# Two layers of linear attention and a Mish MLP: load order and turns at the start, one block's statistics, and the order of the last products

## The chip, the cores and the metric

The kernel runs on one core of a Trainium2 chip. A core has TensorE (PE in the profile, with its weight loads as PEld), VectorE (DVE), ScalarE (ACT), GpSimd (POOL), SyncE (SP, which here issues the DMAs) and 16 DMA engines. SBUF is the working memory of 128 partitions; PE writes its results to PSUM, eight banks of 512 fp32 columns. The metric is the device time of one execution in microseconds; less is better.

## The reference

Input `x` has 2048 rows of 640. Two layers run one after the other with the same weights. Each is an attention part and a dense part with a layer norm ahead and a residual addition behind:

```python
for layer in range(2):
    x = x + attention(layernorm(x))
    x = x + mlp(layernorm(x))

# attention, 32 heads of 20
q, k, v = split_heads(x @ wqkv)
pq, pk = q @ w_phi, k @ w_phi                       # per head, 20 x 20
phi = concat(softmax(p), softmax(-p))               # 40 features, for q and for k
kv, z = phi_k^T @ v, sum(phi_k)                     # over all 2048 rows
o = (phi_q @ kv) / (phi_q . z + 1e-6)
return o @ wo

# mlp
h = x @ w1 + b1                                     # 1536 wide
return (h * tanh(softplus(h))) @ w2
```

All is fp32.

## The kernel before

Rows are taken in `NB` = 8 blocks of 256, each as two row tiles of 128 (`t` = 0, 1). Every large product is made of three: an operand is split into a high part (`ACT` copies it rounded) and a low part (DVE or POOL subtracts), and high by high, high by low and low by high are added up in PSUM. A row of 640 results lies in two halves of 320 columns, `c` = 0, 1, a PSUM bank each. PSUM is given out as two double tiles `mm` (`mm_tile`, two banks each) and four single ones (`one_tile`).

A layer has three stages. `attend_first` runs over the blocks and makes keys, values and queries, and their features; `attend_second` runs over them again for the attention's output; `dense` runs over (block, `pr`) steps, 12 per block. In step `pr`, `hidden` makes two of the twelve times 128 hidden columns, `mish` brings them through the activation on ACT, DVE and POOL to `ah` and `al` (high and low parts), and two steps later `contract` multiplies them by `w2`. `end` adds the row block `xt` and stores it.

The first layer's start is written out by hand, on all engines. PE first makes `TURNS` transposes of the identity matrix (L543), whose result nobody reads. SP issues the loads: the first row tile (L549), the first part of the feature map `w_phi` as block diagonals (`load_phi`, L256), the raw transposed query weights in six tiles (`load_raw`, L247), and the rest of the map (three loads, L258 and L260). `differences` (DVE, L266) turns the map into differences to each head's first feature. `fold` (PE, L273) multiplies raw weights and map to folded weights, five products per raw tile, one per 128 rows of the weights; `fold_parts` splits them into high (ACT, L282) and low (DVE, L284). Tile 0 of the raw weights is folded for all five, then tile 1 for two of them, then PE turns the first normalised rows (L355), and then come the rest of tile 1 and tile 2. The values' weights `wv` (L138) and the keys' raw weights are loaded behind.

Further on in the same stretch `fold_keys` folds the keys' weights; their low parts are written `parts[2]` and `parts[3]` in an order of their own. Then come the values of the first block, whose PSUM tiles are those that `parts[3]` held. `norm_stats` (L290, L292) and `norm_scale` (POOL L300 and L301, DVE L305) make mean and scale of a block.

Behind this, from the second block on, only PE's and SP's order is written for a while, or nobody's: a planner that simulates the time puts the instructions in order. `tc.issue_after(ins)` tells it that what is made inside stands behind `ins` on the engine of `ins`. So stand the third block's statistics: `fetch_normed(b + 1)` at `b == 1` stands behind `ready`, which is DVE's last shift of the second block's `norm_scale`:

```python
with tc.issue_after(ready):
    xt = fetch_normed(b + 1)
```

At the end of the last layer, the last `contract` takes its 24 products with the two hidden columns outermost (`j`, then `t`, `c` and the three parts), and the planner may still move them. `end` adds the four results of 128 x 320 one by one on DVE (L994) and stores row tile 0 whole (L998) and row tile 1 in halves (L996).

Of the kernel before, what the change touches and what calls it, by code (L numbers as in the profile page):

```python
# [8 lines left out]
F32 = mybir.dt.float32  # L9
F32R = mybir.dt.float32r  # L10
AF = mybir.ActivationFunctionType
ALU = mybir.AluOpType
# [4 lines left out]
P = 128  # L17
# [6 lines left out]
KF = F // P  # L24
BT = 2
BLK = BT * P
NB = S // BLK
NT = S // P
G = 11
HC = D // 2  # L30
# [7 lines left out]
SKEW = 2  # L38
V_ORDER = (0, 1, 4, 2, 3)
FOLD = (6, 6, 6, 6, 4, 4)  # L40
TURNS = 20
LAYERS = 2
LN_EPS = 1e-5
DEN_EPS = 1e-6
# [7 lines left out]
def kernel(  # L52
# [13 lines left out]
    nc = tc.nc  # L66
# [8 lines left out]
    def mm_tile():  # L75
        return psum.tile([P, 2, 512], F32, tag="mm", name="mm", bufs=2)

    def one_tile():
        return psum.tile([P, 512], F32, tag="one", name="one", bufs=4)
# [4 lines left out]
    def x_tile():  # L84
        return work.tile([P, BT, D], F32, tag="x", name="xt", bufs=2)
# [19 lines left out]
    stats = const.tile([P, NB, 2, BT], F32, name="stats")  # L105
# [10 lines left out]

    last_act = [None]
    written = [False]
    last_scale = [None]
    last_recip = [None]  # L120

    def act(*args, **kw):
# [51 lines left out]
    def r2_wide(j, dtype=F32R):  # L174
        return wts.tile([P, 2, D], dtype, tag=f"r2{j}", name=f"r2{j}")
# [60 lines left out]
    def load_raw(which, ts=range(6)):  # L236

        raw = []
        for t in ts:
            r0 = which * D + DH * sum(FOLD[:t])  # L240
            if t < 5:
                r = wts.tile([P, D], F32, tag=f"r2{'hl'[which]}{5 + t}", name=f"raw{which}{t}")
            else:
                r = row_tile() if which else r2_wide(10, F32)[:, 0]

            n = P if t < 5 else DH * FOLD[t]
            nc.sync.dma_start(r[:n], wqk_t[r0:r0 + n, :])  # L247
            raw.append(r)
        return raw

    def load_phi(bd, late):

        flat = bd.rearrange("p t c -> p (t c)")
        src = phi_bd.rearrange("p t c -> p (t c)")
        if not late:
            nc.sync.dma_start(flat[:, :360], src[:, :360])  # L256
            return
        nc.sync.dma_start(flat[:, 360:600], src[:, 360:600])  # L258
        for n, rows in enumerate((slice(80, 120), slice(0, 40))):
            nc.sync.dma_start(flat[40 * n:40 * n + 40, 600:680], src[rows, 560:640])  # L260
# [17 lines left out]
    def fold_parts(ws, ps, k, c, which=(0, 1)):  # L278
        n0, n1 = (0, 18 * DF) if c == 0 else (18 * DF, FW)
        hi, lo = ws[k][0][:, n0:n1], ws[k][1][:, n0:n1]  # L280
        if 0 in which:
            nc.scalar.activation(hi, ps[:, :n1 - n0], AF.Copy)  # L282
        if 1 in which:
            nc.vector.tensor_tensor(lo, ps[:, :n1 - n0], hi.bitcast(F32), op=ALU.subtract)  # L284

    def norm_stats(t, xt):

# [7 lines left out]
    def norm_scale(b, mvs, t0=0, later=False):  # L295

        n = len(mvs)
        ve = work.tile([P, BT], F32, tag="ve", name="ve", bufs=2)
        for t in range(n):
            nc.gpsimd.tensor_scalar(ve[:, t:t + 1], mvs[t][:, 1:2], LN_EPS, 1.0, op0=ALU.add, op1=ALU.mult)  # L300
        nc.gpsimd.tensor_tensor(stats[:, b, 0, t0:t0 + n], ve[:, :n], neg_half[:, :n], op=ALU.pow)  # L301

        def shifts():
            for t in range(n):
                last_scale[0] = nc.vector.tensor_scalar(stats[:, b, 1, t0 + t:t0 + t + 1], mvs[t][:, 0:1],  # L305
                                                        stats[:, b, 0, t0 + t:t0 + t + 1], -1.0,
                                                        op0=ALU.mult, op1=ALU.mult).ins
        if later:
            return shifts
        shifts()  # L310
# [56 lines left out]
    def row_tile():  # L367
        return work.tile([P, D], F32, tag="xn", name="xn", bufs=4)

    def normed_rows(b, xt):  # L370

        xn = [row_tile() for _ in range(BT)]
        normalize(b, xn, [xt[:, t, :] for t in range(BT)])
        return xn
# [4 lines left out]
    def normalize(b, dst, src):  # L379
        for t in range(BT):  # L380
            act(dst[t], src[t], AF.Identity, bias=stats[:, b, 1, t:t + 1], scale=stats[:, b, 0, t:t + 1])
# [87 lines left out]
    def fetch(x_src, b, xt=None):  # L469
        xt = x_tile() if xt is None else xt  # L470
        nc.sync.dma_start(xt, row_block(x_src, b))
        return xt

    def attend_first(layer, x_src, first):
# [62 lines left out]
        if first is None:  # L537
            E = mybir.EngineType
            with tc.manual_schedule(engines={E.PE, E.SP, E.Activation, E.DVE, E.Pool}):
                written[0] = True  # L540
                ps = one_tile()
                for _ in range(TURNS):
                    nc.tensor.transpose(ps[:, :P], ident, ident)  # L543
                xt = x_tile()
# [3 lines left out]
                def fetch_first(t):  # L548
                    nc.sync.dma_start(xt[:, t], row_block(x_src, 0)[:, t])  # L549
# [8 lines left out]
                def query_parts(banks, c, ks):  # L558
                    for n in range(2):
                        for k in ks:  # L560
# [1 line left out]

                fetch_first(0)
                load_phi(bd, False)
                raw = load_raw(0, range(3))
                load_phi(bd, True)
                raw += load_raw(0, range(3, 6))
                fetch_first(1)
                q_ws = [r2_pair(k) for k in range(KD)]
                kv_ws = [r1_pair(k) for k in range(KD)]  # L570
# [2 lines left out]
                mvs = [norm_stats(0, xt)]  # L573
# [4 lines left out]
                                        op0=ALU.mult, op1=ALU.add)  # L578
# [17 lines left out]
                turned, last = one_tile(), one_tile()  # L596
# [9 lines left out]
                mvs = [norm_stats(1, xt)]  # L606
# [25 lines left out]
                raw = raw_k  # L632
# [15 lines left out]
                xt = fetch(x_src, 1)  # L648
                mvs = [norm_stats(t, xt) for t in range(BT)]
# [1 line left out]
                    for n in range(2):  # L651
                        parts[k](n)
                norm_scale(1, mvs)
                ready = last_scale[0]
                next(g1)
                parts[2](0)
                parts[3](0)
                parts[2](1)
                parts[3](1)
                nxt_rows = normed_rows(1, xt)  # L660
                next(g1)
                next(g0)
# [28 lines left out]
        for b in range(0 if layer else 1, NB):  # L691
            xts = nxt
            order = ("k0", "k1", "v0", "v1", "q0", "q1")
            if b == 0:
                order = ("v0", "k0", "k1", "v1", "q0", "q1")
            elif b == 1 and layer == 0:
                order = ("k0", "q0", "k1", "v0", "q1", "v1")
            elif b == NB - 1:
                order = ("k0", "k1", "v0", "v1", "q0")
            vs = [v_tile() for _ in range(BT)]  # L700
            for n, (kind, t) in enumerate(order):
                t = int(t)
# [6 lines left out]
                if b + 1 < NB:  # L709
                    if n == 0 and b == 1 and layer == 0:  # L710
                        with tc.issue_after(ready):
                            xt = fetch_normed(b + 1)
                    elif n == 0:
                        xt = fetch_normed(b + 1)
# [213 lines left out]
    def dense(x_src, x_dst, w1s, w2s, first, last):  # L928
        blocks = {0: first}
# [38 lines left out]
            nc.gpsimd.tensor_tensor(al[:, js], n, ah[:, js].bitcast(F32), op=ALU.subtract)  # L968

        def contract(b, pr, ah, al):  # L970
            if pr == 0:
                blocks[b][2] = [mm_tile() for _ in range(BT)]
            pys = blocks[b][2]
            order = [(t, j) for t in range(BT) for j in range(2)]
            if b == NB - 1 and pr == KF // 2 - 1:
                order = [(t, j) for j in range(2) for t in range(BT)]
            for t, j in order:
                sl = slice(t * P, (t + 1) * P)
                f = 2 * pr + j
                for c in range(2):  # L980
                    cs = slice(c * HC, (c + 1) * HC)
                    wh, wl = w2s[f][0][:, cs], w2s[f][1][:, cs]
                    for n, (l, r) in enumerate(((ah, wh), (ah, wl), (al, wh))):
                        nc.tensor.matmul(pys[t][:, c, :HC], l[:, j, sl], r,  # L984
                                         start=(f == 0 and n == 0), stop=(f == KF - 1 and n == 2))

        def end(b):
            xt, _, pys = blocks.pop(b)
            dst = row_block(x_dst, b)
            if last and b == NB - 1:  # L990
                for t in range(BT):
                    for c in range(2):
                        cs = slice(c * HC, (c + 1) * HC)
                        nc.vector.tensor_tensor(xt[:, t, cs], pys[t][:, c, :HC], xt[:, t, cs], op=ALU.add)  # L994
                        if t == BT - 1:
                            nc.sync.dma_start(dst[:, t, cs], xt[:, t, cs])  # L996
                    if t < BT - 1:
                        nc.sync.dma_start(dst[:, t], xt[:, t])  # L998
                return
            mvs = []  # L1000
            for t in range(BT):
                nc.vector.tensor_tensor(xt[:, t, :].rearrange("p (c d) -> p c d", c=2), pys[t][:, :, :HC],
                                        xt[:, t, :].rearrange("p (c d) -> p c d", c=2), op=ALU.add)
                if not last:
                    mvs.append(norm_stats(t, xt))
            if not last:
                norm_scale(b, mvs)
            nc.sync.dma_start(dst, xt)
            if not last:
                xn = [row_tile() for _ in range(BT)]  # L1010
                normalize(b, xn, [xt[:, t, :] for t in range(BT)])
                spill_turned(xn, n2_d[b])
# [13 lines left out]
        for i in range(len(steps) + SKEW):  # L1026
            if i < len(steps):
                b, pr = steps[i]
# [19 lines left out]
            if i <= KD:  # L1048
                with tc.issue_after(exps[0]):
                    w = next(last_w2)  # L1050
# [5 lines left out]
            if i >= SKEW:  # L1056
                b, pr = steps[i - SKEW]
# [5 lines left out]
    with tc.block(schedule_with_timeline_sim=True):  # L1063
        src, first = x, None
        for layer in range(LAYERS):
            last = layer == LAYERS - 1
# [5 lines left out]
            w2s = {}  # L1072
# [73 lines left out]
```

## Time and profile before

| | |
|---|---|
| median of 3 runs | 1357.73 us (1356.86 to 1359.12) |
| the profiled execution | 1358.86 us |
| its span | 1357.0 us |
| PE busy | 1349.5 us (99%) |
| DVE busy | 1069.5 us (79%) |
| ACT busy | 584.5 us (43%) |
| POOL busy | 469.3 us (35%) |
| bytes moved by DMA | 169.21 MB, mean 125 GB/s |

The span runs from the first to the last instruction of the program. A row of the timeline gives start and duration in us, engine, line of the kernel, operation, and tiles as out<-in, with the number of merged instructions; in brackets stands how long the engine was idle before, and what ended that. Products overlap in PE, so a row of several lasts longer than their number times their pace. `raw` are raw weights, `big` is here the feature map, `r1h`, `r1l`, `r2h` and `r2l` are weights in parts, `xth` and `xtl` turned rows in parts, `ol` the activated hidden columns.

### The profile page before, as it was taken

How to read it: one execution, taken by the hardware profiler on the slowest of the kernel's cores; microseconds unless marked ns; L12 is line 12 of the kernel's file. 1: busy time of each engine (PE TensorE's matmuls, PEld its weight loads, DVE VectorE, ACT ScalarE, POOL GpSimd, SP SyncE). 2: the span in 40 equal slices, each digit the busy share in tenths (PEclk: the TensorE clock that was granted, in tenths of full speed). 3: DMA queues.
4: the chain of work that ended last, by engine and by line, in shares of the span. 5: the costliest groups of instructions: out<-in, count | busy, mean ns of one | idle time of the engine just before them, and what ended most of it. 6: DMA issues, size and time to landing. Idle time of an engine off the chain costs nothing.

```text
span 1357.0 us, 30926 instructions
## 1 busy us (share of the span) xinstructions
PE 1349.5 (99%) x12886; PEld 1337.6 (99%) x12886; DVE 1069.5 (79%) x1810; ACT 584.5 (43%) x1039; POOL 469.3 (35%) x357
## 2 busy tenths in 40 slices
PE   9999999999999999999999999999999999999998
PEld 9999999999999999999999999999999999999998
DVE  6988788887787887778779888888768776676775
ACT  5443444222454545545444344332236444444443
POOL 3345644444222222222225556744441211111111
PEclk9999999999999999999999999999999999999999
DMA  9624335798614542334473534467964231233200
GB/s 337 183 41 78 81 60 124 186 287 285 192 36 94 117 117 73 60 102 109 133 238 72 115 72 76 82 159 233 301 238 117 79 87 26 85 98 98 73 26 20
DMA packets 350613, 169.21 MB, mean 125 GB/s; under 512 B 287225, under 2 KB 323817, under 8 KB 350473
## 3 DMA queue, kind: packets, MB, share of 16 engines
q1 hardware_dynamic: 350473, 167.23, 46.2%
q8 instruction: 101, 1.65, 0.5%
q14 instruction: 39, 0.32, 0.1%
HBM read 104.61 MB, written 62.59 MB: 123 GB/s over the span
## 4 chain that ended last, share of the span: by engine, by line
PE 98%; DVE 1%; DMA 0%; ACT 0%; issue 0%; SPq 0%; DVEq 0%; ACTq 0%
PE mm L417 28%; PE mm L984 25%; PE one L942 25%; PE one L417 13%; PE mm L802 3%; PE one L327 2%; PE one L502 2%; PE mm L273 0%; DMA raw<-in_wqk_t 0%; DVE r1l L284 0%; PE one L802 0%; DVE m L453 0%; DVE r L458 0%; DVE r L456 0%; PE one L273 0%
## 5 line engine op out<-in xcount | busy, mean ns | idle before, releaser
L984 PE MATMUL mm<-r2h,ol 128*128 128x320 f32 x1280 | 304.9, 309 | 0.0
L968 POOL TENSOR_TENSOR ol<-big,ol 128x512 fp32r<-128x512 f32 (+1 forms) x98 | 130.5, 1332 | 484.7 <-ACT ol L967 391.3
L942 PE MATMUL one<-xtl,r1h 128*128 128x256 f32 x960 | 268.6, 280 | 0.0
L942 PE MATMUL one<-xth,r1l 128*128 128x256 f32 x960 | 268.4, 280 | 0.0
L942 PE MATMUL one<-xth,r1h 128*128 128x256 f32 x960 | 266.3, 280 | 0.0
L984 PEld LDWEIGHTS mm<-r2h,ol 128*128 128x128 f32 x1280 | 219.4, 188 | 0.0
L984 PE MATMUL mm<-r2l,ol 128*128 128x320 f32 x640 | 197.6, 310 | 0.0
L417 PE MATMUL mm<-r1h,xth 128*128 128x304 f32 (+1 forms) x600 | 185.3, 309 | 0.0
L417 PE MATMUL mm<-r1h,xtl 128*128 128x304 f32 (+1 forms) x600 | 184.1, 307 | 0.0
L417 PE MATMUL mm<-r1l,xth 128*128 128x304 f32 (+1 forms) x600 | 183.9, 306 | 0.0
L942 PEld LDWEIGHTS one<-xtl,r1h 128*128 128x128 f32 x960 | 180.8, 188 | 0.0
L942 PEld LDWEIGHTS one<-xth,r1l 128*128 128x128 f32 x960 | 180.7, 188 | 0.0
L942 PEld LDWEIGHTS one<-xth,r1h 128*128 128x128 f32 x960 | 179.9, 188 | 0.0
L957 DVE TENSOR_SCALAR big<-big 128x512 f32<-128x512 f32 (+1 forms) x98 | 56.2, 573 | 112.1 <-ACT big L955 111.9
L466 POOL TENSOR_TENSOR big<-big,r 128x1280 f32<-128x1280 f32 x42 | 101.4, 2418 | 70.3 <-DVE r L465 46.1
L984 PEld LDWEIGHTS mm<-r2l,ol 128*128 128x128 f32 x640 | 120.4, 188 | 0.0
L955 ACT ACTIVATE big<-one,b1s 128x256 f32<-128x256 f32 x192 | 80.8, 467 | 91.7 <-PE one L942 90.8
L959 ACT ACTIVATE big<-big,two 128x512 f32<-128x512 f32 (+1 forms) x98 | 70.1, 716 | 115.2 <-DVE big L958 115.0
L967 ACT ACTIVATE ol<-big 128x512 fp32r<-128x512 f32 (+1 forms) x98 | 60.9, 621 | 133.4 <-DVE big L966 133.2
L417 PEld LDWEIGHTS mm<-r1h,xth 128*128 128x128 f32 x600 | 113.0, 188 | 0.6
L417 PEld LDWEIGHTS mm<-r1h,xtl 128*128 128x128 f32 x600 | 112.9, 188 | 0.4
L417 PEld LDWEIGHTS mm<-r1l,xth 128*128 128x128 f32 x600 | 113.0, 188 | 0.0
(171 smaller groups left out, 3121.1 us busy)
## 6 DMA issues: line engine op xcount, KB each, us to landing
big<-e_d SPq DMA_DIRECT2D x30, 640.0 KB, 6.4
x_d<-xt SPq DMA_DIRECT2D x23, 640.0 KB, 4.2
e_d<-r SPq DMA_DIRECT2D x88, 160.0 KB, 4.0
xt<-x_d SPq DMA_DIRECT2D x22, 640.0 KB, 5.9
n_d<-xn SPq DMA_DIRECT2D x176, 80.0 KB, 2.2
xt<-in_x SPq DMA_DIRECT2D x15, 640.0 KB, 4.4
xn<-x_d SPq DMA_DIRECT2D x28, 320.0 KB, 4.6
v<-n_d SPq DMA_DIRECT2D x30, 256.0 KB, 3.2
```

What stands on the lines that cost most here:

```text
L327: nc.tensor.transpose(ps[:, c, t * P:(t + 1) * P], self.rows[t][:, (c0 + c) * P:(c0 + c + 1) * P], ident)
L417: nc.tensor.matmul(ps[:, :w], a[:, sl], r, start=(k == 0 and n == 0), stop=(k == final and n == end))
L466: nc.gpsimd.tensor_tensor(eg, eg, r.unsqueeze(2).to_broadcast([P, 2 * H, DH]), op=ALU.mult)
L502: nc.tensor.matmul(kva[32 * q:32 * q + DH + 1, c:c + 2 * DH], v[:, (DH + 1) * h:(DH + 1) * (h + 1)], e[:, 2 * DH * h:2 * DH * (h + 1)], st ...
L802: nc.tensor.matmul(po[c][64 * q:64 * q + 64, GW * j:GW * j + w], phs[g][:n, s0:s0 + 64], kvb[:n, g, :w], start=True, stop=True)
L942: nc.tensor.matmul(ph[:, j, :], l, r, start=(n == 0), stop=(n == 3 * KD - 1))
L955: exps[0] = nc.scalar.activation(part(ta, 0)[:, j - js.start], ph[:, j, :], AF.Exp, bias=b1s[:, 2 * pr + j:2 * pr + j + 1]).ins
L957: nc.vector.tensor_scalar_min(e, e, E_CAP)
L959: nc.scalar.activation(r, n, AF.Ln, bias=two)
L967: nc.scalar.activation(ah[:, js], n, AF.Copy)
L968: nc.gpsimd.tensor_tensor(al[:, js], n, ah[:, js].bitcast(F32), op=ALU.subtract)
L984: nc.tensor.matmul(pys[t][:, c, :HC], l[:, j, sl], r, start=(f == 0 and n == 0), stop=(f == KF - 1 and n == 2))
```

## The change

Four edits. The number of turns at the start goes from 20 to 24. The three loads of the map's rest are issued behind the first raw tile instead of behind the third. `ready` becomes DVE's last low part of the keys' `parts[2]` and `parts[3]`, so that the third block's statistics stand behind it. In the last block of the last layer, row tile 1's second half gets a PSUM tile of its own (`one_tile`, held for the block's 12 steps), the last 24 products get a written order, row tile 0 first with the low parts of its second hidden column last, then the first half of row tile 1, then its second half, and `end` reads from the tile of its own.

```diff
-TURNS = 20
+TURNS = 24
...
-    last_scale = [None]
+    last_low = [None]
...
         if 1 in which:
-            nc.vector.tensor_tensor(lo, ps[:, :n1 - n0], hi.bitcast(F32), op=ALU.subtract)
+            last_low[0] = nc.vector.tensor_tensor(lo, ps[:, :n1 - n0], hi.bitcast(F32), op=ALU.subtract).ins
...
-                last_scale[0] = nc.vector.tensor_scalar(stats[:, b, 1, t0 + t:t0 + t + 1], mvs[t][:, 0:1],
-                                                        stats[:, b, 0, t0 + t:t0 + t + 1], -1.0,
-                                                        op0=ALU.mult, op1=ALU.mult).ins
+                nc.vector.tensor_scalar(stats[:, b, 1, t0 + t:t0 + t + 1], mvs[t][:, 0:1],
+                                        stats[:, b, 0, t0 + t:t0 + t + 1], -1.0, op0=ALU.mult, op1=ALU.mult)
...
-                raw = load_raw(0, range(3))
+                raw = load_raw(0, range(1))
                 load_phi(bd, True)
-                raw += load_raw(0, range(3, 6))
+                raw += load_raw(0, range(1, 6))
...
                 norm_scale(1, mvs)
-                ready = last_scale[0]
                 next(g1)
                 parts[2](0)
                 parts[3](0)
                 parts[2](1)
                 parts[3](1)
+                ready = last_low[0]
                 nxt_rows = normed_rows(1, xt)
...
         def contract(b, pr, ah, al):
+            final = last and b == NB - 1
             if pr == 0:
                 blocks[b][2] = [mm_tile() for _ in range(BT)]
+                if final:
+                    blocks[b].append(one_tile())
             pys = blocks[b][2]
-            order = [(t, j) for t in range(BT) for j in range(2)]
+
+            def product(t, j, c, n):
+                f = 2 * pr + j
+                l, w = ((ah, 0), (ah, 1), (al, 0))[n]
+                ps = blocks[b][3] if final and t == c == 1 else pys[t][:, c]
+                nc.tensor.matmul(ps[:, :HC], l[:, j, t * P:(t + 1) * P], w2s[f][w][:, c * HC:(c + 1) * HC],
+                                 start=(f == 0 and n == 0), stop=(f == KF - 1 and n == 2))
+
+            order = [(t, j, c, n) for t in range(BT) for j in range(2) for c in range(2) for n in range(3)]
             if b == NB - 1 and pr == KF // 2 - 1:
-                order = [(t, j) for j in range(2) for t in range(BT)]
...
+                order = [(t, j, c, n) for j in range(2) for t in range(BT) for c in range(2) for n in range(3)]
+                if final:
+                    order = ([(0, 0, c, n) for c in range(2) for n in range(3)] + [(1, 0, 0, n) for n in range(3)]
+                             + [(0, 1, c, n) for ns in ((0, 1), (2,)) for c in range(2) for n in ns]
+                             + [(1, 1, 0, n) for n in range(3)] + [(1, j, 1, n) for j in range(2) for n in range(3)])
+            with ExitStack() as written_order:
+                if final and pr == KF // 2 - 1:
+                    written_order.enter_context(tc.manual_schedule(engines={mybir.EngineType.PE}))
+                for o in order:
+                    product(*o)
...
-                        nc.vector.tensor_tensor(xt[:, t, cs], pys[t][:, c, :HC], xt[:, t, cs], op=ALU.add)
+                        ps = apart[0] if t == c == 1 else pys[t][:, c]
+                        nc.vector.tensor_tensor(xt[:, t, cs], ps[:, :HC], xt[:, t, cs], op=ALU.add)
```

More of the change, by code (lines that the diff above doesn't have):

```diff
@@ L970, in contract @@
         def contract(b, pr, ah, al):
+            final = last and b == NB - 1
             if pr == 0:
                 blocks[b][2] = [mm_tile() for _ in range(BT)]
+                if final:
+                    blocks[b].append(one_tile())
             pys = blocks[b][2]
-            order = [(t, j) for t in range(BT) for j in range(2)]
-            if b == NB - 1 and pr == KF // 2 - 1:
-                order = [(t, j) for j in range(2) for t in range(BT)]
[L977 to L985, printed above, removed]
+            def product(t, j, c, n):
[4 more added lines that the diff above has]
+                                 start=(f == 0 and n == 0), stop=(f == KF - 1 and n == 2))
@@ L987, in end @@
+            with ExitStack() as written_order:
[3 more added lines that the diff above has]
+                    product(*o)
         def end(b):
-            xt, _, pys = blocks.pop(b)
+            xt, _, pys, *apart = blocks.pop(b)
             dst = row_block(x_dst, b)
```

## The prediction

> **What bounds the kernel now.** I read the page first, then who waits for whom on PE, then the timeline of the three places that the diff touches. The page says that PE is busy nearly everywhere and that the chain that ended last is PE's own.
>
> ```profile
> PE 1349.5 (99%) x12886; PEld 1337.6 (99%) x12886; DVE 1069.5 (79%) x1810; ACT 584.5 (43%) x1039; POOL 469.3 (35%) x357
> ```
>
> ```profile
> PE 98%; DVE 1%; DMA 0%; ACT 0%; issue 0%; SPq 0%; DVEq 0%; ACTq 0%
> ```
>
> The waits of PE (engine, line, what it waited for, us in total, times, longest) show what little an edit could remove inside the span, beside PE's late start.
>
> ```profile
> PE one L273 <- DMA raw<-in_wqk_t: 0.6, 1, 0.6
> ...
> PE one L417 <- DVE r1l L284: 0.4, 1, 0.4
> ```
>
> In the steady stretch the chain (start, us, what) has a step of the dense layer as 30 hidden and 24 final products, 3.50 + 3.52 = 7.02 us, and a product of 320 columns at 3.52 / 24 = 0.147 us.
>
> ```profile
> 1331.47 3.50 PE one L942 x30
> 1334.97 3.52 PE mm L984 x24
> ```
>
> So no edit of this kind is worth tens of microseconds. What can be won is at the front, where PE waits and runs slowly, in one stall near 36 us, and behind the last product. The reader is to see in the next rows (start, duration, engine, line, tiles, count) that the same eight fold products take 1.92 us at 7.04 and 1.06 us at 11.32.
>
> ```profile
> 1.34 4.53 PE L543 MATMUL one<-ident 128*128 128x128 f32 x20 [1.34 <-POOL ident masks.py:199]
> 1.67 1.30 SPq L247 DMA_DIRECT2D raw<-in_wqk_t  x3
> 3.01 0.44 SPq L258 DMA_DIRECT2D big<-in_phi_bd  x1
> 3.49 0.71 SPq L260 DMA_DIRECT2D big<-in_phi_bd  x2
> ...
> 6.50 0.75 PE L273 MATMUL one<-big,raw 120*128 120x114 f32 x2 [0.63 <-DMA raw<-in_wqk_t]
> 7.04 1.92 PE L273 MATMUL mm<-big,raw 120*128 120x114 f32 x8
> ...
> 9.60 1.00 PE L355 MATMUL one<-ident,xn 128*128 128x128 f32 x5
> ...
> 11.32 1.06 PE L273 MATMUL mm<-big,raw 120*128 120x114 f32 x8
> ```
>
> The products' own durations (ns, minimum, median, most) are these.
>
> ```profile
> L273 PE MATMUL mm<-big,raw x70: 243/276/422, 7.0 to 31.3; 120*128 120x114 f32 x56, 80*128 80x76 f32 x14
> ```
>
> So one product follows the other after (1.92 - 0.42) / 7 = 0.214 us, and later after (1.06 - 0.28) / 7 = 0.112 us. The five turns of 9.60 would take 1.28 us at the slow pace and 0.72 at the fast one; with 1.00 the step lies among them, at about 10.2 us. PE ran at half pace for all of its first nine microseconds, the 20 turns included, although the page's clock row reads full speed.
>
> **Edits 1 and 2: 24 turns, late maps ahead of the second raw weights.** Four more turns cost 4 x 0.214 = 0.86 us of PE. The 20 end at 5.87, and as the next instruction can follow 0.21 before that, 24 let the first fold start at 5.87 - 0.21 + 0.86 = 6.52, where it starts at 6.50 today. They lie wholly in the wait for the first raw weights; if those land sooner, because only 138 KB of maps and no longer 640 KB of raw weights share the DMA engines with them, the turns cost what the landing gains. I count nothing for that.
>
> What the turns can bring is the pace. 4.3 us of unbroken turns (1.34 to 5.66) were not enough to raise it, and 3.7 us of work from 6.50 to 10.2 were. So the pace isn't counted from the first instruction. [...]
>
> [...]
>
> Then the ten products of the first raw tile: 1.8 slow ones to 6.9, 8.2 x 0.112 = 0.92 behind, done at 7.82. The second raw tile is wanted there; today it isn't wanted before 8.75. Its landing, with those of the third and the fourth, follows (KB, us from issue to landing; two issued with steps of 0.43 in the group of 1.67, at 2.1 and 2.5, the other behind the maps, at 4.2), and the DMA rate in the last column of the stretch.
>
> ```profile
> raw<-in_wqk_t SPq DMA_DIRECT2D x1, 320.0 KB, 5.4
> ```
>
> ```profile
> raw<-in_wqk_t SPq DMA_DIRECT2D x1, 320.0 KB, 5.8
> ```
>
> ```profile
> raw<-in_wqk_t SPq DMA_DIRECT2D x1, 320.0 KB, 6.0
> ```
>
> ```profile
> 7.50:8.50 1.00, 1.00 (x6) 1.00 (x6) 0.00 (x0) 0.00 (x0) 0.00 (x0) 1.00 1.05 391
> ```
>
> It lands at 7.5 today, the third at 8.3, the fourth at 10.2. On SP the three map loads now pass ahead of the second and third raw load, which are issued 0.44 + 0.71 = 1.15 us later; that alone doesn't move a landing that comes 5.4 us after the issue. 138 KB at 391 GB/s put it 0.35 us later. From above: between the landings of the third and the fourth lie 1.9 us for the maps and one raw tile that elsewhere takes 0.8 to 1.1 us, so the maps can cost 1.1 us. I take 0.45, nearer the row of the rate, as the small map loads overlap others: 7.95. PE stands for 0.1 us. From 8.0 follow 4 products (0.45), 5 turns (0.55) and 16 products (1.79), to 10.8, where today this ends at 12.2. Gain 1.45 us; by the ends (check at 8.0; raw tile at 8.6) 0.8 to 1.5. That this isn't given back at once is seen in what comes next.
>
> ```profile
> 13.65 0.74 ACT L143 ACTIVATE r1h<-xn 128x640 fp32r<-128x640 f32 x1 [0.18 <-DMA xn<-in_wv]
> ...
> 17.09 0.92 ACT L125 ACTIVATE xn<-xt,stats 128x640 f32<-128x640 f32 x1 [1.96 <-DVE stats L305]
> ...
> 18.06 0.77 PE L355 MATMUL one<-ident,xn 128*128 128x128 f32 x5
> ```
>
> ACT's high parts ahead of these rows wait for PE's folds and move with them. ACT's copy of 13.65 waits for a load that doesn't move, so ACT gives back 1.3 us there, but between it and the normalised row of 17.09 stand 1.96 us of idle ACT, which cover it. The row then comes with DVE's statistics, as early as PE.
>
> **Edit 3: the third block's statistics.** In the rows DVE is full, and PE's values wait for its low parts, whose reads free a PSUM bank.
>
> ```profile
> 31.81 1.66 DVE L290 BATCH_NORM_STATS2 bn<-xt 128x6 f32<-128x320 f32 x4
> ...
> 34.12 0.27 DVE L292 BATCH_NORM_AGGREGATE mv<-bn 128x2 f32<-128x12 f32 x2
> ...
> 35.76 0.84 DVE L284 TENSOR_TENSOR r1l<-one,r1h 128x342 fp32r<-128x342 f32 x2
> ...
> 38.62 0.79 DVE L284 TENSOR_TENSOR r1l<-mm,r1h 128x342 fp32r<-128x342 f32 x2
> ```
>
> ```profile
> 35.92 0.31 PE L417 MATMUL one<-r1h,xtl 128*128 128x320 f32 x1
> 36.66 0.42 PE L417 MATMUL one<-r1h,xth 128*128 128x320 f32 x1 [0.43 <-DVE r1l L284]
> 36.91 0.31 PE L417 MATMUL one<-r1l,xth 128*128 128x320 f32 x1
> ```
>
> The diff lets the helper's DVE work follow the last low part of 35.76 instead of the second block's shift. Four statistics and two aggregates, 1.66 + 0.27 = 1.93 us, go behind it, and the low parts end at 34.67 instead of 36.60. PE wants the bank 0.147 us after 35.92, at 36.07, so the wait goes: 36.66 - 36.07 = 0.59, and the first product behind it takes 0.25 instead of 0.15, together 0.69 us. From below nothing is excluded: if the planner puts other work in that place, 0. The block's load stands on SP, which the wait doesn't touch. The moved work delays the last low parts of 38.62 by nothing, as all of it stood ahead of them before. What is late next: POOL's two steps behind the aggregates and then DVE's shifts, ahead of POOL's long products.
>
> ```profile
> 34.41 0.99 POOL L300 TENSOR_SCALAR ve<-mv 128x1 f32<-128x1 f32 x2 [4.75 <-DVE mv L292]
> 35.48 0.70 POOL L301 TENSOR_TENSOR stats<-ve,neg_half 128x2 f32<-128x2 f32 x1
> 38.93 2.37 POOL L466 TENSOR_TENSOR r<-r,r 128x1280 f32<-128x1280 f32 x1 [2.75 <-DVE r L465]
> ```
>
> These 1.69 us fit into POOL's 2.75 idle us ahead of 38.93 if DVE is done with the aggregates by about 37; then they cost nothing.
>
> **Edit 4: the last products by row tile.** The last product, the four additions and the stores:
>
> ```profile
> 1352.00 1.68 DVE L994 TENSOR_TENSOR xt<-mm,xt 128x320 f32<-128x320 f32 x4 [3.53 <-PE mm L984]
> ...
> 1352.24 0.31 PE L984 MATMUL mm<-r2h,ol 128*128 128x320 f32 x1
> 1352.91 0.34 SPq L998 DMA_DIRECT2D out<-xt  x1
> 1353.31 0.91 SPq L996 DMA_DIRECT2D out<-xt  x2
> ```
>
> Today the four additions stand in a row from 1352.00, a pace of 0.40, and the last ends at 1353.68, 1.13 behind PE's end (1352.55). After the change the first row tile is done 9 products of 0.147 us, 1.32 us, before the end; its two additions and the third one (its bank is done 6 products, 0.88 us, before the end) are through by 1351.27 + 3 x 0.40 = 1352.47. The last starts at about 1352.6 and ends at 1353.08; the last store goes with it. Gain 0.60 to 0.68, the larger by the last store's issue (1353.77 against 1353.09); I take 0.65. It isn't more, as the store's own flight stays. The written order needs the second half's parts earlier, and holds a fourth bank for the block:
>
> ```profile
> 1337.19 0.88 DVE L962 SCALAR_TENSOR_TENSOR big<-one,b1s,big 128x256 f32<-128x256 f32 x2
> ```
>
> ```profile
> 1347.32 0.87 POOL L968 TENSOR_TENSOR ol<-big,ol 128x256 fp32r<-128x256 f32 x1 [4.46 <-issue]
> ...
> 1348.99 0.74 POOL L968 TENSOR_TENSOR ol<-big,ol 128x256 fp32r<-128x256 f32 x1 [0.81 <-ACT ol L967]
> ```
>
> The last 24 products start at 1352.39 - 24 x 0.147 = 1348.9. The first low part (1348.19) is wanted by the third of them, the second (1349.73) by the fourteenth, at 1350.8. Both are there. A bank of hidden products is read last at 1338.07, 6.6 us after its group began, and three banks come round in 3 x 7.02 = 21 us: nothing.
>
> **The sum.** 1.45 + 0.69 + 0.65 = 2.8 us. The profiled execution took 1358.86 (span 1357.0 and 1.86 around it) and would take 1356.1. It lies 1.13 above the median of the runs, 1357.73; from that, 1354.9.
>
> **The rivals.** First, the pace comes no sooner: the turns don't count, or raw weights leave a new hole. Then edit 1 brings about 0.1, and the time is 1357.73 - 0.1 - 1.34 = 1356.3. For it: 20 turns, 4.3 us, raised nothing. Against it: the step at 10.2 fell among turns.
>
> [...]
>
> Second, the stall of edit 3 comes back at the next DVE product, block 1's third low part, or where PE waits for the bank through something else: 1354.9 + 0.7 = 1355.6.
>
> ```profile
> 50.76 0.41 DVE L333 TENSOR_TENSOR xtl<-one,xth 128x256 fp32r<-128x256 f32 x1
> ```
>
> Block 1's keys start on PE at 50.8 and want it 1.8 us later, so 1.4 us of room are left, 0.7 after the change. Against the rival is that room.
>
> Third, slower: DVE's shift of the third block stands in its queue ahead of that low part and waits for POOL, where the two steps come behind both long products, 2 x 2.37 = 4.7 us. PE then stands for 4.7 - 0.7 = 4.0, and the time is 1354.9 + 4.0 = 1358.9. It is slower than before from a wait of 3.5 us on. Against it: POOL is idle for 2.75 us just then.
>
> **How the numbers follow.** The forecast has a chance of 0.58 (its own range 1354.0 to 1355.8), the first rival 0.16, the second 0.09, the third 0.06. 0.11 go to the planner, which times anew all stretches whose order isn't written, from the second block on: 0.06 better, 0.05 worse, each by some 2 us or more. About 0.2%, 2.7 us, is what a measurement of this kernel can tell from no change; the bound is 1355.0. Of the forecast 0.42 lie below it, with the better plan 0.48 are faster; the rest of it, the first two rivals and half of the third make 0.43 or slightly less; slower 0.10. The range takes in the first rival and part of the third: 1353.2 to 1358.0.
>
> **What would show it.** Right: fold products at 0.112 us from about 7 us on and the last of them ending near 10.8; no wait of PE on line 284's work; statistics of the third block behind 35; the last addition ending 0.5 us after the last product, alone. Wrong: slow products still at 9 us, a wait of PE for the second raw tile over 0.5 us, DVE waiting for POOL's statistics before 50, or PE waits in layer 2 that are not there now.

## The result and the profile after

| | before | after |
|---|---|---|
| median of 22 runs each | 1357.93 us | 1356.09 us |
| lowest to highest | 1356.03 to 1359.35 | 1354.68 to 1357.96 |
| the profiled execution | 1358.86 | 1356.78 |
| its span | 1357.0 | 1355.0 |
| from the end of PE's last product to the end of the span | 4.48 | 3.74 |

The ratio of the runs is 0.9986, with a 95% interval of 0.9980 to 0.9992: 1.8 us less where 2.8 was forecast. The time lies within the range of 1353.2 to 1358.0, but 0.3 us outside the forecast's own range (1354.0 to 1355.8) and next to the first rival's 1356.3. The change is smaller than the 0.2% that the prediction took as its bound, but the whole interval lies below 1.

In the changed kernel the lines of the dense part and of `features` have moved by one to three, those of `end` by eleven. PE's waits (engine, line, what it waited for, us in total, times, longest):

```profile
PE one L542 <- POOL ident masks.py:199: 1.3, 1, 1.3
PE mm L416 <- DVE xtl L332: 0.5, 1, 0.5
PE mm L801 <- issue: 0.4, 1, 0.4
PE one L416 <- ACT r1h L143: 0.3, 1, 0.3
```

The waits for the raw weights and for line 284's low parts are gone, and two that were not there before have come: for `xtl` of line 332, and for the value weights' high parts, line 143. PE's pace is here the time from one product's start to the next one's. At the front, in the timeline of the changed kernel, all turns are slow (0.213 us from one to the next) and the folds fast (0.112) nearly from their first:

```profile
1.34 5.38 PE L542 MATMUL one<-ident 128*128 128x128 f32 x24 [1.34 <-POOL ident masks.py:199]
6.52 0.50 PE L273 MATMUL one<-big,raw 120*128 120x114 f32 x2
6.86 1.06 PE L273 MATMUL mm<-big,raw 120*128 120x114 f32 x8
7.75 0.39 PE L273 MATMUL one<-big,raw 120*128 120x114 f32 x2
...
9.63 1.06 PE L273 MATMUL mm<-big,raw 120*128 120x114 f32 x8
```

The last group of folds of the first three raw tiles starts at 9.63 instead of 11.32, 1.69 us earlier. The statistics of the third block now stand at 34.98, behind the low parts, and those of the fourth at 45.55:

```profile
32.83 0.85 DVE L284 TENSOR_TENSOR r1l<-one,r1h 128x342 fp32r<-128x342 f32 x2
...
34.98 1.67 DVE L290 BATCH_NORM_STATS2 bn<-xt 128x6 f32<-128x320 f32 x4
...
43.41 1.51 DVE L514 STREAM_TRANSPOSE r<-r 128x1280 f32<-128x1280 f32 x1 [1.57 <-POOL r L465]
45.55 1.67 DVE L290 BATCH_NORM_STATS2 bn<-xt 128x6 f32<-128x320 f32 x4 [0.64 <-DMA xt<-in_x]
47.15 0.33 DVE L292 BATCH_NORM_AGGREGATE mv<-bn 128x2 f32<-128x12 f32 x2
47.39 1.23 DVE L332 TENSOR_TENSOR xtl<-one,xth 128x512 fp32r<-128x512 f32 x2
...
50.40 0.41 DVE L332 TENSOR_TENSOR xtl<-one,xth 128x256 fp32r<-128x256 f32 x1
```

```profile
50.08 0.30 PE L416 MATMUL mm<-r1l,xth 128*128 128x304 f32 x1
50.87 0.41 PE L416 MATMUL mm<-r1h,xtl 128*128 128x304 f32 x1 [0.48 <-DVE xtl L332]
```

DVE waits there 0.64 us for the load of the fourth block's rows, and before that 1.57 us for POOL, in front of the second block's last low part, and PE stands behind that. At the end:

```profile
1349.93 1.29 DVE L1005 TENSOR_TENSOR xt<-mm,xt 128x320 f32<-128x320 f32 x3 [2.80 <-PE mm L981]
1351.25 0.49 DVE L1005 TENSOR_TENSOR xt<-one,xt 128x320 f32<-128x320 f32 x1
```

```profile
1350.90 0.31 PE L981 MATMUL one<-r2h,ol 128*128 128x320 f32 x1
```

Three additions are through when PE's last product ends (1351.21), and one stands behind it. Where the time of the two profiled executions went is found from the start of the same PE instruction in both (after minus before, us):

| place in the program | PE earlier by |
|---|---|
| first fold | -0.02 |
| last fold of the first three raw tiles | 1.69 |
| first block's values done, at 41 us before | 2.38 |
| second block's keys, at 53 us | 1.63 |
| last dense step of the first layer, at 667 us | 1.60 |
| around the second layer's first values, at 696 us | 1.10 |
| second layer's attention output, at 931 us | 1.34 |
| end of PE | 1.34 |
| end of the span | 2.08 |

So 2.4 us were won by 41 us, more than the 2.1 of the forecast's two terms; 0.75 was given back at 50, 0.5 at 690, and 0.24 came back near 914. The last row has what the end of the kernel adds, 0.74.

### The profile page after: what moved, and what is told of

It reads as the page before. It is cut to its first block, busy times and chain, and to the rows that moved or that the text cites. A ratio compares the mean times of both kernels' runs of the same rounds, so it can differ in the third digit from the quotient of the medians.

```text
span 1355.0 us, 30935 instructions
## 1 busy us (share of the span) xinstructions
PE 1348.6 (100%) x12890; PEld 1336.9 (99%) x12890; DVE 1069.8 (79%) x1810; ACT 584.7 (43%) x1039; POOL 469.3 (35%) x357
## 4 chain that ended last, share of the span: by engine, by line
PE 98%; DMA 1%; DVE 1%; issue 0%; ACT 0%; POOL 0%; SPq 0%; POOLq 0%; DVEq 0%; ACTq 0%
PE mm L416 27%; PE one L941 25%; PE mm L981 24%; PE one L416 13%; PE mm L801 3%; PE one L326 2%; PE one L501 2%; PE mm L273 1%; DMA xt<-in_x 1%; DMA v<-in_wv 0%; PE one L542 0%; PE one L981 0%; PE one L273 0%; PE one L801 0%; DVE bn L290 0%
## 5 line engine op out<-in xcount | busy, mean ns | idle before, releaser
L981 PE MATMUL mm<-r2h,ol 128*128 128x320 f32 x1260 | 301.3, 309 | 0.0
L981 PEld LDWEIGHTS mm<-r2h,ol 128*128 128x128 f32 x1260 | 216.0, 188 | 0.0
L981 PE MATMUL mm<-r2l,ol 128*128 128x320 f32 x630 | 194.3, 309 | 0.0
```

Source lines behind the costliest of these rows:

```text
L981: nc.tensor.matmul(ps[:, :HC], l[:, j, t * P:(t + 1) * P], w2s[f][w][:, c * HC:(c + 1) * HC], start=(f == 0 and n == 0), stop=(f == KF - 1 ...
```

## The experiments

Three questions were open: whether the faster folds come from the edits at all; whether the stall's 0.69 us stays or is taken by the wait at 50; what the own bank is worth in the last edit. A hole is the time in which PE is idle between its last turn and the first fold; the tail is the time from the end of PE's last product to the end of the span. The first four kernels ran on one chip beside one set of runs of the kernel before (median 1357.18), the next four beside another (1357.49), the last four beside a third (1357.34).

### The parts of edits 1 and 2

```diff
-TURNS = 24
+TURNS = 20
```

> The changed kernel with 20 turns instead of 24. Theory (a hole in PE's work ahead of the first fold delays the faster pace): the turns end at 5.87, the first raw tile lands at about 6.1 (the load that waits for it is issued at 6.12 in the changed kernel), so a hole of about 0.45 us opens ahead of the first fold, about half that of the kernel before. Either it is small enough, and folds run at 0.112 us from 7 on and the time is 1356.1 as with 24, or it isn't, they run at 0.214 until about 10, and the median is up to 1.3 us higher, 1357.4. Rival (the turns only fill time, the new load order made the folds fast): fast folds from 7 on, 1356.1 or 0.3 less, as the first fold can start 0.4 us earlier.

The median was 1355.94 against 1357.18 of the kernel before beside it, ratio 0.9989 (0.9980 to 0.9997).

```profile
1.34 4.12 PE L542 MATMUL one<-ident 128*128 128x128 f32 x20 [1.34 <-POOL ident masks.py:199]
6.16 0.45 PE L273 MATMUL one<-big,raw 120*128 120x114 f32 x2 [0.70 <-DMA raw<-in_wqk_t]
```

The hole is there, 0.70 us. But 20 turns take 4.12 us, not 4.53: the last of them ran at the fast pace already, from 4.97 us on, and the hole didn't take it away. The expectation had not reckoned with fast turns.

```diff
-                raw = load_raw(0, range(1))
+                raw = load_raw(0, range(3))
                 load_phi(bd, True)
-                raw += load_raw(0, range(1, 6))
+                raw += load_raw(0, range(3, 6))
```

> The changed kernel with the late maps behind the third raw tile again. Theory (the 24 turns carry edit 1 and 2): they end at 6.72, after the first raw tile's landing (6.4), so no hole opens, folds run at 0.112 us from 7 on, the second raw tile lands sooner, and the median is the same, 1356.1 within 0.4. Rival (the load order carries it): slow folds until 10, 1357.4 or more.

1355.62, ratio 0.9989 (0.9980 to 0.9998): the same as with the new order. The pace stepped at 5.45, and the first fold started at 6.21.

### Edit 3 and the wait behind it

```diff
                 norm_scale(1, mvs)
+                ready = last_scale[0]
...
-                ready = last_low[0]
```

> The changed kernel with the third block's statistics ahead of the key low parts again. Theory A (the end of the stretch is set by the load of the fourth block's rows, which DVE waits for at 45.5 and PE behind it at 50): PE waits again 0.6 to 0.7 us near 34 us and no longer or less near 50, and the median is 1356.1 to 1356.3. Theory B (edit 3's 0.69 us is a gain of its own): 1356.8, with both waits.

1356.33, ratio 0.9995 (0.9986 to 1.0004).

```profile
33.97 0.31 PE L417 MATMUL one<-r1h,xtl 128*128 128x320 f32 x1
35.10 0.42 PE L417 MATMUL one<-r1h,xth 128*128 128x320 f32 x1 [0.82 <-DVE r1l L285]
```

The stall is back, 0.99 us beyond the usual 0.15, and no wait at 50. In this profile that looks like theory A. But the wait at 50 was also absent in the profiles of the two kernels above, which have edit 3, so it isn't the price of it. The median is 0.4 to 0.7 above theirs, as theory B has it; the intervals overlap. So the stall is back at about the size that the forecast gave it; that the median moves by as much fits, but these intervals don't show it. What was given back at 50 in the first profile was one execution's late landing of a load.

```diff
+            if b == 1:
+                second = xts
...
-                    elif n == 0:
+                    elif n == 0 and b == 2 and layer == 0:
+                        with tc.issue_after(second.done):
+                            xt = fetch_normed(b + 1)
+                    elif n == 0:
                         xt = fetch_normed(b + 1)
```

> The changed kernel with the fourth block's statistics put behind the second block's last low part on DVE. Theory A (DVE stood in line for the load of the fourth block's rows, ahead of that low part): PE's wait near 50 us of 0.76 us goes, and the median is 1355.3 to 1355.5. Theory B (the low part is late for POOL's sake or for DVE's own work): a wait of at least 0.4 us stays there, 1355.7 to 1356.1. Theory C (PE comes earlier, but meets the loads of the second layer's value weights near 690 us, where it now waits 0.5 us): the wait at 50 goes and that at 690 grows, 1355.7 to 1356.1.

1355.60, ratio 0.9990 (0.9981 to 0.9999): not better than the others.

```profile
47.80 0.42 DVE L332 TENSOR_TENSOR xtl<-one,xth 128x256 fp32r<-128x256 f32 x1
48.13 1.67 DVE L290 BATCH_NORM_STATS2 bn<-xt 128x6 f32<-128x320 f32 x4
```

The low part comes at 47.80 instead of 50.40 and nobody waits at 50. As that wait comes only now and then, the edit has little to remove. Two other waits stood in its profile, one of 0.5 us for the value weights (theory C) and one of 1.6 us that none of the theories has:

```profile
PE mm L806 <- issue: 1.6, 1, 1.6
PE one L542 <- POOL ident masks.py:199: 1.3, 1, 1.3
PE one L416 <- ACT r1h L143: 0.5, 1, 0.5
```

### Edit 4

```diff
-            final = last and b == NB - 1
+            final = False
...
-                        ps = apart[0] if t == c == 1 else pys[t][:, c]
+                        ps = apart[0] if apart and t == c == 1 else pys[t][:, c]
```

> The changed kernel with the last products, their PSUM tiles and the additions as before. Everything ahead is in the same order. Theory: from PE's last product to the end of the span it is 4.4 to 4.5 us again instead of 3.8, and the median is 0.65 us higher, 1356.75. Rival (the order of the products costs PE time that the tail gave back): 1356.1 to 1356.4.

1357.02 against 1357.49 of the kernel before, ratio 0.9994 (0.9985 to 1.0003). The span ends at 1356.6 and PE's last product at 1351.83 + 0.31 = 1352.14: a tail of 4.5 us, as before the change, where all kernels with the whole edit have 3.7 to 3.8.

```profile
1351.59 1.68 DVE L1005 TENSOR_TENSOR xt<-mm,xt 128x320 f32<-128x320 f32 x4 [3.53 <-PE mm L981]
```

The order without the bank:

```diff
-                if final:
-                    blocks[b].append(one_tile())
...
-                ps = blocks[b][3] if final and t == c == 1 else pys[t][:, c]
+                ps = pys[t][:, c]
...
-                        ps = apart[0] if t == c == 1 else pys[t][:, c]
+                        ps = pys[t][:, c]
```

> The changed kernel with the written order of the last products, but row tile 1's second half in the double tile as before. Theory (the bank of its own lets the third addition start while PE still writes row tile 1): the third addition waits for PE's end, two additions of 0.40 us stand behind it, and the tail behind PE's last product is 4.2 us. Rival (the order alone does it): 3.8 us.

One execution: 1354.65, a span of 1352.8, PE's end at 1348.95, a tail of 3.87.

```profile
1347.67 0.89 DVE L1003 TENSOR_TENSOR xt<-mm,xt 128x320 f32<-128x320 f32 x2 [2.80 <-PE mm L979]
1348.99 0.89 DVE L1003 TENSOR_TENSOR xt<-mm,xt 128x320 f32<-128x320 f32 x2 [0.43 <-PE mm L979]
```

The third addition waits for PE's end as expected, and the last one ends 0.93 us behind PE's last product, where it is 0.53 with the bank. But the tail is only 0.1 us longer, not 0.4: the rival was nearer, and in this one execution the order alone brings 0.6 of the 0.7. So the last addition alone doesn't set the end of the span; what else does was not taken apart.

### What sets PE's pace

```diff
-TURNS = 24
+TURNS = 40
```

> The changed kernel with 40 turns. Theory (turns count as work for PE's pace): their pace steps from 0.214 to 0.11 us among themselves, between 4.7 and 8.2 us, and the 40 take 6.0 to 8.0 us instead of 8.9; folds run fast from their first. Rival (turns don't count): all 40 run at 0.214 us and take 8.9 us, and the folds behind them start slow and get fast about 3.7 us later.

```profile
1.34 6.28 PE L542 MATMUL one<-ident 128*128 128x128 f32 x40 [1.34 <-POOL ident masks.py:199]
7.46 0.38 PE L273 MATMUL one<-big,raw 120*128 120x114 f32 x2
```

40 turns take 6.28 us and not 8.9; from about 4.9 us on they follow each other at 0.11. The pace stepped up here with nothing but turns ahead. The time was 1357.54 in its one execution: the folds start at 7.46, about 1 us too late. With one turn (`TURNS = 1`):

> The changed kernel with one turn. [...] Rival (the pace follows the time since the start and not the work): fast before 8 us as with 24.

```profile
6.00 0.74 PE L273 MATMUL one<-big,raw 120*128 120x114 f32 x2 [4.19 <-DMA raw<-in_wqk_t]
6.54 1.91 PE L273 MATMUL mm<-big,raw 120*128 120x114 f32 x8
...
9.10 1.03 PE L354 MATMUL one<-ident,xn 128*128 128x128 f32 x5
```

Slow until 9.74, 3.7 us behind the first fold, and 1359.11 us in its one execution. This is the front of the profile of before, although that had 20 turns.

### The two halves, and the kernel before once more

> The kernel before, profiled once more. Theory P (its profiled execution was an unlucky one: in seven of the eight looks with 20 to 40 turns of the changed kernel and its variants the pace stepped up at 4.6 to 5.6 us, among the turns, ahead of where the hole opens): the pace steps up at about 5 us among the 20 turns, the last fold of the first three raw tiles ends near 10.6 instead of 12.4, and the span is about 1.5 us shorter, 1355.5. Theory Q (the hole delays the pace in most executions of the kernel before): the step comes near 10 us again, span 1357.

```profile
1.34 3.80 PE L543 MATMUL one<-ident 128*128 128x128 f32 x20 [1.34 <-POOL ident masks.py:199]
5.51 0.45 PE L273 MATMUL one<-big,raw 120*128 120x114 f32 x2 [0.37 <-DMA raw<-in_wqk_t]
5.80 1.06 PE L273 MATMUL mm<-big,raw 120*128 120x114 f32 x8
```

The kernel before, unchanged, stepped up at 4.32 us here, and its folds were fast from the first: a span of 1354.1 instead of 1357.0. 2.14 us of the difference lie at the front. Its stall was there, with 0.6 us of wait for line 284, and its tail of 4.5.

```profile
34.66 0.41 PE L417 MATMUL one<-r1h,xth 128*128 128x320 f32 x1 [0.57 <-DVE r1l L284]
```

Edits 3 and 4 alone (20 turns and the old load order in the changed kernel):

> The changed kernel with 20 turns and the old load order: edits 3 and 4 alone. Theory P: the pace steps up at about 5 us; the median is as with all four edits, within 0.4 us, some 1.3 us below the kernel before (0.73 of the tail, 0.6 of the stall). Theory Q: slow folds to about 10 us, and a median 1 us or more above that of all four.

```profile
1.34 4.23 PE L542 MATMUL one<-ident 128*128 128x128 f32 x20 [1.34 <-POOL ident masks.py:199]
6.38 0.45 PE L273 MATMUL one<-big,raw 120*128 120x114 f32 x2 [0.81 <-DMA raw<-in_wqk_t]
6.67 1.06 PE L273 MATMUL mm<-big,raw 120*128 120x114 f32 x8
```

A hole of 0.81 us, wider than that of the first profile (0.63), ahead of fast folds: the pace had stepped up at 5.19. Edits 1 and 2 alone (24 turns and the new load order in the kernel before):

> The kernel before with 24 turns and the late maps behind the first raw tile: edits 1 and 2 alone. Theory P: nothing measurable, within 0.5 us of the kernel before, as the folds start at 6.1 to 6.5 and were fast anyway. Theory Q: 1.0 to 1.7 us faster. In both the stall near 36 us is there, and 4.5 us of tail.

All four beside them:

> The changed kernel, on the same chip as the two halves. Theory P: its gain on the kernel before (0.9986 on another chip, 1.9 us) is that of edits 3 and 4 alone, 1.3 us or a little more. Theory Q: it is the sum of two like halves, 1 us and 1.3 us.

| kernel | median us | ratio to before (1357.34, 27 runs) | tail us |
|---|---|---|---|
| edits 1 and 2 | 1357.93 | 1.0002 (0.9993 to 1.0011) | 4.5 |
| edits 3 and 4 | 1355.58 | 0.9983 (0.9974 to 0.9992) | 3.75 |
| all four | 1355.59 | 0.9986 (0.9978 to 0.9995) | 3.76 |

Edits 3 and 4 bring all that can be measured. For edits 1 and 2 the interval runs from 0.95 us faster to 1.5 us slower: the 1.45 us of the forecast lie outside it, half a microsecond doesn't. To that extent theory P holds. For edits 3 and 4 it runs from 1.1 to 3.5 us faster, where the forecast had 1.34.

Of PE's other waits, these two show how much an execution can differ by chance: with edits 1 and 2 PE stood 1.8 us in a wait without a releaser near 912 us, in the changed kernel's first profile 0.4.

```profile
914.01 0.69 PE L802 MATMUL mm<-kvb,xt 120*64 120x63 f32 x16 [1.83 <-issue]
```

```profile
913.56 0.68 PE L801 MATMUL mm<-kvb,xt 120*64 120x63 f32 x16 [0.40 <-issue]
```

The page counts the DMA queue that loads instructions:

```profile
q8 instruction: 101, 1.65, 0.5%
```

Its 101 packets have 16,384 bytes each. Nine of the fourteen profiles have a wait near this place. In the first profile of before PE goes on at 915.01, 1.57 us behind the landing of one of these packets (913.44); in the first of after it goes on at 913.56, 1.62 us behind one (911.94). As an estimate from these times PE may wait there for its next instructions; the profile names no releaser, and why the wait is longer in some executions stays open.

## Why the prediction was right, and where it was not

The direction held and the time lay in the range. But of the sum of 1.45 + 0.69 + 0.65 the first term doesn't show in the runs, and the forecast itself, 1354.9, was 1.2 us too low. That the time lay in the range is owed to its width, which took in the first rival.

**Edits 1 and 2, 1.45 us forecast.** In the two first profiles this looked exact: 1.69. As a term of the median it was wrong: measured alone, the two edits give 1.0002. The pace stepped up at these times in the executions profiled here (us, from the single starts of PE's products):

| turns | pace steps up at |
|---|---|
| 1 | 9.74 |
| 20 | 10.22 (the first profile of before), 4.32, 4.97, 5.19 |
| 24 | 6.71 (the first profile of after), 5.45, 4.59, 5.61, 5.24, 4.97, 5.88, 7.12 |
| 40 | 4.81 |

The trace also keeps the full clock as a record with a start, which the rows of the profile don't print. It starts at 10.18 us in the first profile of before and at 6.77 in that of after, within 0.07 us of the step in the table.

No run shows the 6.9 us that the forecast took for the moment of the step, nor the 8.0 us at the end of its range, as a moment that holds for every execution: in the profiles the step lay between 4.32 and 10.22. With 24 turns two of the eight had it near 6.9, at 6.71 and 7.12, and that the first profile of after is one of them is luck. Beside the first profile of before, with its hole of 0.63 us and its step at 10.22, this one has the folds over 1.69 us earlier; that the hole kept the pace down was the author's estimate. It fits these two executions and that with one turn (4.19 us of idle PE, the step at 9.74); but with 24 turns the step lies anywhere from 4.59 to 7.12, so single executions don't show it. The step that failed is the last one, where the term found in one profile is taken off the median ("It lies 1.13 above the median of the runs, 1357.73; from that, 1354.9"), as if the pace stepped up at one place in every execution. It stepped up between 4.32 and 5.88 in ten of the thirteen profiles with 20 turns or more, among the turns; there a hole behind the step takes nothing away, as with 0.70 and 0.81 us ahead of fast folds in two of those with 20 turns. In the other three it came at 6.71, 7.12 and 10.22. As an estimate from these counts, up to 1.7 us in three executions of thirteen are 0.4 us on the mean at most, and the runs of edits 1 and 2 alone can't tell that from nothing. The profiled execution's 1.13 us above the median hinted at it.

**The landing of the second raw tile, forecast at 7.95 with 0.1 us of stand.** Nobody waited: in the changed kernel the products of the second tile start at 7.75 without a gap, so the tile was there by then.

**Edit 3, 0.69 us.** Right as to the wait: that for line 284 stands in all profiles without the edit (0.4 to 0.8 us) and in none with it. What is late next was named in the second rival, the second block's third low part, with 0.7 us of room left. That room was gone in the first profile, as PE came 2.4 us earlier there while the low part came only 0.36 earlier. The forecast's 0.7 us of room had both move by the 1.45 us of the front. Two things held DVE back: its wait for POOL's long product, which is 1.54 to 1.57 us in nine of the ten profiles with edit 3 and 0.72 or 0.73 in the four without it, and the load of the fourth block's rows, 0.64 us, which doesn't move with PE. POOL's part is there each time and cost PE nothing by itself; DVE's wait for the load was 0.3 us or nothing in the other executions with edit 3 and 24 turns.

**Edit 4, 0.65 us.** 0.73 in all profiles: 4.48 to 3.75. The last addition starts 0.04 behind the last product's end and not 0.05, and the last store is issued with it; a size off by a tenth. The own bank, to which the forecast gave the third addition, brought only 0.1 of it in the one execution without the bank.

**The rivals.** The first (1356.3: the pace comes no sooner) came nearest to 1356.09, but for another reason: in most executions the pace comes no sooner because it is early in both kernels. Its mechanism, that turns don't count, is refuted by the 40 turns, where the step came at 4.81 us with nothing but turns ahead; among the turns it also came in nine of the other twelve profiles with 20 turns or more. The third rival, DVE behind POOL, came in part, as told under edit 3: in the last profile of all four edits DVE's wait for POOL is 1.56 us, and PE waits nowhere near 50.

**The signs.** All that was to show the forecast right stood in the first profile: fast folds from 6.86 on, the last of them over by 10.7, no wait for line 284, the third block's statistics at 34.98, one addition behind the last product. Of the signs of being wrong one came too, a PE wait in the second layer that wasn't there before, of 0.3 us. None of them could tell whether the median has the first term. The chances, too, add up to 1.01: by the parts given, no change has 0.44 and slower 0.08.

**Given back elsewhere.** PE waits 0.3 to 0.9 us for the second layer's value weights near 690 in eight of the eleven profiles of the changed kernel and its variants, and not in the two of the kernel before or that of edits 1 and 2 alone. PE's being earlier isn't enough to explain it, as the second profile of before was as early; the cause stays open. The waits near 912 appear with and without the edits, from nothing to 1.8 us, and single profiles differ by as much for that alone.

## What to carry to other kernels

Where an engine's pace steps up at a moment that differs from execution to execution, a profile shows one draw: take the same kernel's profile again before a gain is read from it, and compare halves of the change on one chip. A gain that hangs on such a moment counts only for the share of executions in which the moment falls there. The gain behind the last product of the bounding engine (here the order of the last results) was the same 0.73 us in every profile; those ahead of it could be taken back by loads that don't move, as at 50.

## What was not expected of the hardware

The kernel before raised PE's pace 3.0 us after PE's first instruction in one execution (1.34 to 4.32) and 8.9 us after it in another (10.22). Behind the step the pace stayed through holes of 0.37, 0.70 and 0.81 us (20 turns: the second profile of before, the changed kernel, edits 3 and 4). The profile's clock row read full speed at the slow and the fast pace alike, 0.213 and 0.109 us from one turn to the next in the first profile of before: ahead of 10.18 us its trace has no clock record, and the row shows 1.00. The products' own times show the step, and so does the start of the record.
